# Tile 3's v moved behind the second quarter of w_in, with a planner told of later landings, in a fused local attention and squared-ReLU FFN kernel

## The chip, the cores and the metric

The kernel runs on one core of a Trainium2 chip. The metric is the device time of one execution in microseconds (us); lower is better. The core's engines run their own instruction streams and meet through semaphores: TensorE (PE in the profile; its weight loads are PEld), VectorE (DVE), ScalarE (ACT), GpSimd (POOL) and SyncE (SP). POOL, SP and ACT also issue DMA transfers, which the core's 16 DMA engines carry out.

## The reference, cut to what matters

```python
batch, n_heads, seq, head_dim = (4, 8, 768, 64)
n_global, n_local = (8, 96)
n_tokens, d_model, d_ff = (3072, 512, 2048)

scores = q @ k.T / sqrt(64)                       # per batch and head
rel = pos[:, None] - pos[None, :]
is_global = pos[None, :] < n_global
is_local = (rel >= 0) & (rel < n_local)
keep = is_global | is_local
dist = where(is_global & ~is_local, n_local, abs(rel))
scores = where(keep, scores - slope[head] * dist, -1e9)
a = softmax(scores)
x = (a @ v) as [3072 tokens, 512]                 # heads side by side
h = maximum(x @ w_in, 0)                          # w_in is 512 x 2048
out = (h * h) @ w_out                             # w_out is 2048 x 512
```

All inputs and the output are float32. The kernel works in float16 and accumulates in float32.

## The kernel before

**Tiling.** The 3072 tokens are cut into 24 tiles of 128; six tiles make one of the four sequences. A query looks at most 95 keys back and at the first 8 keys of its sequence, so a tile needs its own keys, those of the tile ahead of it (into which `fix_k` and `fix_v` copy the global keys and values) and nothing else. Attention runs tile by tile. The two layers of the FFN run on chunks, `CHUNKS = [1]*8+[2]*8`: chunks c0 to c7 are one tile each, c8 to c15 two tiles each (c9 is tiles 10 and 11).

**One tile's chain.** q and k are transposed to head-major form: in tiles 0 to 5 by TensorE (`trp`, then a copy to `qk` by `evac`), later by a DMA transpose that SP issues (L422). TensorE makes the scores `sp` (L466; 16 matmuls for the two key tiles, 8 in the first tile of a sequence), ACT takes the exponential to `ex` (L479), DVE multiplies by the mask to `ph` (L485), TensorE multiplies with v to `av` (L495), and DVE divides (`rec`, `tm`; L504 and L505). `tm` is transposed to `xt`: in tiles 0 to 5 by TensorE (`trx`, L511) and a copy, from tile 6 on by a DMA transpose on SP (L523).

**The FFN.** Layer 1 (`first`, L639) goes over 16 slices m of w_in, 128 columns each, with four matmuls per slice into `hps`; slices m0 to m3 need the first quarter of w_in, m4 to m7 the second, and so on. ACT takes the ReLU (`hr`, L647), DVE squares it (`h`, L654). Layer 2 (`second`, L660) makes `yps` in four parts, one for each quarter of w_out; DVE copies to `y`, and SP issues the store (L670).

**Loads.** All of q, k, v, w_in and w_out come by DMAs that POOL issues (L359, L395, L402), which also turn float32 to float16; only tile 0's q and k come by SP and ACT. POOL's order is the list in the last block: v of tile 0, then tiles 1 and 2, the first quarter of w_in, tile 3, the other three quarters of w_in, w_out, and the tiles from 4 on. A load waits until its buffer is free (three for q and k together, five for v).

**PSUM.** Two pools: `one`, four buffers of one bank, and `big`, two buffers of two banks. `trp`, `trx`, `av`, `yps` live in `one`; `sp` lives in `big`; `hps` lives where `home` says. A buffer is given out again in turn, when its reader has let it go.

**What sets the order.** The whole program is a list of operations with estimated durations, needs, buffers and ranks. `Plan.emit` walks through it in model time and picks for each engine the next operation whose needs are met, by rank; the pick fixes the instruction order on that engine, and on the chip each engine runs its own order, waiting at an instruction whose input is missing. `late` adds a lag to the modelled landing of POOL's loads; `SURE` and `SLACK` say how much earlier a buffer must be free, and how much later an operation may start, to be among those that are picked from; `NUDGE` shifts ranks of single stages. Where the plan foresees that TensorE idles in the first 45 us it puts in matmuls on zeros (`warm`, L269), which fill the time and compute nothing.

Of the kernel before, what the change touches and what calls it, by code (L numbers as in the profile page):

```python
# [8 lines left out]
FP32 = mybir.dt.float32  # L9
# [4 lines left out]
P = 128  # L14


class Dma:
# [34 lines left out]
class Plan:  # L52
# [115 lines left out]
                gone[key] = done  # L168

    def late(self, at):  # L170
        return 700 if at < 15500 else 1300 if at < 43000 else 0


SURE = {"PE": 0, "ACT": 60, "DVE": 60}
SLACK = {"PE": 0, "ACT": 100, "DVE": 0}


@with_exitstack
def kernel(
# [11 lines left out]
    nc = tc.nc  # L191
# [18 lines left out]
    EARLY = True  # L210


    NUDGE = {('attention', 11): -10, ('attention', 1): 10, ('attention', 13): -10, ('attention', 7): 100, ('layer 2', 1): 25, ('layer 2', 6): 100, ('attention', 8): 10, ('layer 2', 11): -100, ('attention', 3): 10, ('layer 1', 9): -100, (3.5, 1): 100, ('attention', 20): -25, (2.5, 2): 200, (2, 9): -100, ('attention', 6): 10, (4.5, 16): 25, ('layer 2', 13): -200, ('attention', 23): -200, (1.5, 4): -25, ('layer 1', 5): -10, ('layer 1', 10): -10, ('attention', 5): -200, (4, 16): -100, ('layer 2', 0): 50, ('attention', 19): -10, (2, 4): 25, ('attention', 14): 200, ('attention', 9): 50, ('layer 1', 1): 100, (2, 15): -10, (6, 11): -10, ('attention', 18): -10, ('layer 2', 15): 10, ('attention', 2): -100, ('layer 1', 0): 50, (1.5, 8): 100, (3, 3): 200, ('layer 1', 11): -50, (6, 4): 10, ('layer 1', 2): -25, ('layer 2', 8): 50, ('attention', 10): 25, (1.5, 9): 100, (4.5, 4): -10, ('layer 1', 8): 10, (4.5, 7): 100, ('layer 1', 14): 100, ('layer 1', 13): -25}

    EARLY_QK, TOUCH = ("SP","ACT"), "ACT"

    EARLY_V = None

    W_IN = 4


    ADDED = 0
# [1 line left out]
    SPLIT = {}  # L224
# [31 lines left out]
    touched = const.tile([P, NCT, 1], FP32, name="touched")  # L256
    w_out_sb = const.tile([P, NFT, d_model], FP16, name="w_out_sb")


# [14 lines left out]
    add = plan.op  # L274
# [47 lines left out]
    def constants():  # L322
        add("DVE", 120, lambda: vec.memset(blank, 0.0), rank=-999)
        add("DVE", 250, lambda: vec.tensor_scalar(
            out=ident, in0=dist[:, 0:P], scalar1=0.0, scalar2=None, op0=ALU.is_equal),
            needs=["dist"], makes=["ident"], rank=-999)
        if EARLY:
            add("DVE", 250, lambda: vec.tensor_scalar(
                out=ident32, in0=dist[:, 0:P], scalar1=0.0, scalar2=None, op0=ALU.is_equal),
                needs=["dist"], makes=["ident32"], rank=-998)  # L330
        add("DVE", 2350, fill_reach, needs=["dist"], makes=["reach"], rank=-997)
        if ADDED:
            for h in range(H):
                add("ACT", 190, lambda h=h: fill_diag(h), needs=["ident"], makes=[("diag", h)],
                    rank=-990 + h)
        for h in range(H):
            add("ACT", 420, lambda h=h: fill_mask(h), needs=["reach"], makes=[("mask", h)],
                rank=-990 + h if h < 4 else -185)


    v_bufs = [const.tile([P, H, D + 1], FP16, name=f"v{i}") for i in range(BUFS["v"])]
# [40 lines left out]
    def fetch_early_v():  # L382
        queue = {"ACT": nc.scalar, "SP": nc.sync}[EARLY_V[0]]
        add(EARLY_V[0], 450, lambda: queue.dma_start(out=early[:, 2], in_=source(0, "v")),
            makes=["ev"], rank=-998, work=920, to=210, back=1000)
        add(EARLY_V[1], 450, lambda: copy(EARLY_V[1], v_bufs[0][:, :, 0:D], early[:, 2]),
            needs=["ev", "ones"], makes=[("sv", 0)], takes=[("v", ("v", 0))], rank=-100)


    def touch_w_in():  # L390
        {"ACT": nc.scalar, "SP": nc.sync}[TOUCH].dma_start(out=touched, in_=moe_w_in[:, 0:1].rearrange("(k p) f -> p k f", p=P))

    def load_w_in(c):
        n = d_ff // W_IN
        pool_dma(745, lambda: nc.gpsimd.dma_start(  # L395
            out=w_in_sb[:, :, c * n:(c + 1) * n],
            in_=moe_w_in[:, c * n:(c + 1) * n].rearrange("(k p) f -> p k f", p=P)),
            10240 // W_IN if W_IN == 4 else 1340, makes=[("w_in", c)])

    def load_w_out(c):  # L400
        n = NFT // 4
# [127 lines left out]
    def attention(t, c, j, n, due):  # L529
# [5 lines left out]
        if t >= TURN_QK:  # L535
            add("SP", 1230, lambda: turn_by_dma(t), needs=[("sq", t), ("sk", t)],
                work=1920, to=1100, back=1000, takes=[("qk", ("qk", t))], frees=[("stage", t)], rank=due(0),
                makes=all_of("qk", t))
        else:
            for names in (("q", "k") if t == 0 else ("qk",)):  # L540
                for p in parts:
                    add("PE", 56 * len(names) * wide * (2 if t == 0 and EARLY else 1),
                        lambda names=names, p=p: turn(t, p, names),
                        needs=[("s" + x, 0, p) if t == 0 and EARLY else ("s" + x, t) for x in names]
                        + ["ident32" if t == 0 and EARLY else "ident"]
                        + ([("t", t, p, "q")] if names == "k" else []),
                        makes=[("t", t, p, names[-1])],
                        takes=[("one", ("t", t, p))] if "q" in names else [],
                        frees=[("stage", t)] if "k" in names and p == parts[-1] else [], rank=due(0))
            for p in parts:  # L550
                for x in ("qk", ) if t or not SPLIT else "qk":
                    eng = {0: 'DVE', 1: 'DVE', 2: 'DVE', 5: 'DVE', 4: 'DVE', 3: 'DVE'}.get(t, "ACT") if len(x) == 2 else SPLIT[x, parts.index(p)]
# [52 lines left out]
        for p in parts:  # L605
            tms = [("tm", t, g) for g in range(2) if len(parts) == 1 or p == parts[g]]
            takes = [("xt", ("xt", c))] if j == 0 and p[0] == 0 else []
            if t >= TURN_X:
# [4 lines left out]
            add("PE", 56 * wide, lambda p=p: to_x(t, p), needs=tms + ["ident"],  # L613
                makes=[("tx", t, p)], takes=[("one", ("tx", t, p))],
                frees=[("tm", t)] if p == parts[-1] else [], rank=due(4))
            eng = {(1, 0): 'DVE'}.get((t, parts.index(p)), "ACT")
            add(eng, 70 + (70 if eng == "DVE" else 105) * wide, lambda p=p, eng=eng: copy_x(t, c, j, p, eng),
                needs=[("tx", t, p)] + (all_of("x", t - 1) if j else [])
                + ([("x", t, parts[0])] if p != parts[0] else []),
# [4 lines left out]
        return 1 if t0 < 12 else 2  # L624

    def home(t0):
        return "one" if t0 in (0,) else "big"

    def first(c, t0, n, m):
        per = 4 // n  # L630
# [41 lines left out]
    def layer_1(c, t0, n, due):  # L672
        xs = [y for t in range(t0, t0 + n) for y in all_of("x", t)]
        per, x = 4 // n, banks(t0)
        for m in range(NFT):
            i, place = divmod(m, x * per)
            add("PE", 4 * (n * 54 + 1), lambda m=m: first(c, t0, n, m),
                needs=xs + [("w_in", m * W_IN // NFT)] + ([("l1", c, m - 1)] if m else []),
                makes=[("l1", c, m)],
                takes=([(home(t0), ("hps", c, i))] if place == 0 else [])  # L680
                + ([("h2", ("h2", c))] if m == 0 else []),
# [34 lines left out]
    with tc.manual_schedule():  # L716
# [6 lines left out]
            fetch_early()  # L723
        if EARLY_V:
            fetch_early_v()
        if TOUCH:
            add(TOUCH, 530, touch_w_in, rank=-1000, work=460, to=210, back=1000)
        for kind, n in [('v', 0), ('qkv', 1), ('qkv', 2), ('i', 0), ('qkv', 3), ('i', 1), ('i', 2), ('i', 3), ('o', 0), ('o', 1), ('o', 2), ('o', 3), ('qkv', 4), ('qkv', 5), ('qkv', 6), ('qkv', 7), ('qkv', 8), ('qkv', 9), ('qkv', 10), ('qkv', 11), ('qkv', 12), ('qkv', 13), ('qkv', 14), ('qkv', 15), ('qkv', 16), ('qkv', 17), ('qkv', 18), ('qkv', 19), ('qkv', 20), ('qkv', 21), ('qkv', 22), ('qkv', 23)]:
# [51 lines left out]
```

## Time and profile before

| | us |
|---|---|
| median of three runs | 215.76 |
| lowest and highest | 215.57, 215.81 |
| the profiled execution, by the same clock | 214.87 |
| its span, first to last instruction | 213.1 |
| TensorE busy, the `warm` matmuls among it | 205.6 |
| DVE busy | 122.1 |
| ACT busy | 102.7 |
| POOL busy | 68.1 |

The span is 1.77 us shorter than the profiled execution's own time. A row of a timeline reads: start, length, engine, source line, operation, output<-inputs, number of instructions, and in brackets the engine's idle time before and what ended it. The lengths of TensorE's rows hold the drain of the last matmul, so neighbouring rows overlap; the distance between two starts is what the first one takes. The granted clock of TensorE was 0.998 of full speed over the whole span.

### The profile page before, as it was taken

Reading aid. Unit: us, or ns where it says so; the run is one execution under the profiler, and the core shown is the slowest. Engines: PE = TensorE matmul, PEld = TensorE weight load, DVE = VectorE, ACT = ScalarE, POOL = GpSimd, SP = SyncE. Lnnn points to the kernel's source line nnn. Section 1 sums busy time; section 2 is a strip of 40 time slices with the busy share of each in tenths; the row PEclk is TensorE's granted clock in tenths of the full one; section 3 lists DMA queues with packets and bytes.
Section 4 is the critical chain, followed back from the end, with each engine's and each line's share of the span. In section 5 each row is a group of like instructions: output and inputs, shape, how many; then the busy total and the mean of one; then the engine's idle time right before and its main releaser. Section 6 shows DMA issues by size and latency. Waiting matters only on the chain.

```text
span 213.1 us, 5399 instructions
## 1 busy us (share of the span) xinstructions
PE 205.6 (96%) x2253; PEld 145.6 (68%) x2253; DVE 122.1 (57%) x296; ACT 102.7 (48%) x132; POOL 68.1 (32%) x84
## 2 busy tenths in 40 slices
PE   7869999999999999999999999999999999999994
PEld 4458986657967665875878585757676574888453
DVE  5697562774647877657566545664646674232321
ACT  4775663433764656565464635453353641345100
POOL 8975433727604544632207230451000000000000
PEclk9999999999999999999999999999999999999999
DMA  8999999999996999999939999699511222100112
GB/s 121 150 174 205 207 207 173 182 150 253 154 166 127 163 185 203 183 136 205 173 67 98 137 127 134 115 148 179 105 25 52 77 69 82 49 0 3 49 49 98
DMA packets 112232, 27.61 MB, mean 130 GB/s; under 512 B 104784, under 2 KB 109264, under 8 KB 112208
## 3 DMA queue, kind: packets, MB, share of 16 engines
q0 software_dynamic: 77024, 13.37, 87.3%
q1 hardware_dynamic: 33600, 13.64, 30.7%
q10 hardware_dynamic: 1584, 0.26, 0.7%
q8 instruction: 17, 0.28, 0.5%
q14 instruction: 7, 0.06, 0.1%
HBM read 27.27 MB, written 6.29 MB: 157 GB/s over the span
## 4 chain that ended last, share of the span: by engine, by line
PE 90%; DMA 4%; POOL 3%; DVE 1%; issue 0%
PE yps L660 40%; PE hps L639 39%; PE sp L466 5%; PE av L495 5%; DMA w_in_sb<-in_moe_w_in_dram 4%; POOL s L359 2%; POOL v L359 1%; PE trp L416 1%; PE trx L511 0%; DVE qk L429 0%; DVE tm L505 0%; PE warm L269 0%; DVE rec L504 0%; DVE y L429 0%; DVE v L442 0%
## 5 line engine op out<-in xcount | busy, mean ns | idle before, releaser
L639 PE MATMUL hps<-xt,w_in_sb 128*128 128x128 f16 (+1 forms) x1024 | 91.7, 246 | 1.0 <-DMA w_in_sb<-in_moe_w_in_dram 1.0
L660 PE MATMUL yps<-w_out_sb,h 128*128 128x512 f16 (+2 forms) x416 | 91.2, 363 | 0.0
L639 PEld LDWEIGHTS <-w_in_sb 128*128 128x128 f16 x1024 | 79.2, 98 | 12.7 <-DMA w_in_sb<-in_moe_w_in_dram 1.2
L647 ACT ACTIVATE hr<-hps 128x512 f16<-128x512 f32 (+1 forms) x72 | 52.7, 739 | 68.5 <-PE hps L639 64.9
L660 PEld LDWEIGHTS <-h 128*128 128x128 f16 x416 | 37.0, 98 | 34.8 <-DVE h L654 0.4
L654 DVE TENSOR_TENSOR h<-hr 128x512 f16<-128x512 f16 (+1 forms) x72 | 36.7, 511 | 38.8 <-ACT hr L647 38.6
L479 ACT ACTIVATE ex<-sp 128x1024 f16<-128x1024 f32 (+1 forms) x45 | 42.9, 1002 | 20.0 <-PE sp L466 19.9
L359 POOL DMA_DIRECT2D v<-in_v_dram x24 | 21.5, 896 | 64.1 <-issue 19.7
L485 DVE TENSOR_TENSOR ph<-ex,mask 128x1024 f16<-128x1024 f16 (+1 forms) x45 | 30.0, 676 | 14.1 <-ACT ex L479 13.9
L429 DVE COPY y<-yps 128x512 f32<-128x512 f32 (+2 forms) x26 | 16.9, 648 | 20.0 <-PE yps L660 19.7
L359 POOL DMA_DIRECT2D s<-in_q_dram x23 | 20.5, 891 | 7.9 <-PE hps L639 2.4
L359 POOL DMA_DIRECT2D s<-in_k_dram x23 | 20.7, 898 | 4.6 <-DMA w_out_sb<-in_moe_w_out_dram 2.9
L505 DVE TENSOR_TENSOR tm<-av,rec 128x256 f16<-128x256 f32 x48 | 20.4, 424 | 1.7
L495 PE MATMUL av<-v,ph 128*128 128x65 f16 x352 | 15.0, 193 | 1.0 <-DVE ph L485 1.0
L466 PEld LDWEIGHTS <-qk 64*128 64x128 f16 x352 | 9.9, 94 | 8.7 <-issue 5.9
L495 PEld LDWEIGHTS <-ph 128*128 128x128 f16 x352 | 13.6, 97 | 3.1 <-DVE ph L485 1.4
L466 PE MATMUL sp<-qk 64*128 64x128 f16 x352 | 14.2, 218 | 0.5 <-DVE qk L429 0.2
L504 DVE RECIPROCAL rec<-av 128x4 f32<-128x4 f32 x48 | 8.5, 176 | 9.3 <-PE av L495 9.2
L269 PE MATMUL warm<-blank 128*128 128x256 f16 x37 | 7.7, 317 | 1.2 <-DVE v L345 1.2
L439 DVE COPY qk<-qk 128x128 f16<-128x128 f16 x16 | 4.8, 302 | 1.2 <-PE sp L466 0.6
L427 ACT COPY xt<-trx 128x512 f16<-128x512 f16 (+1 forms) x6 | 3.1, 515 | 4.9 <-PE trx L511 4.9
L269 PEld LDWEIGHTS <-blank 128*128 128x128 f16 x37 | 3.8, 113 | 2.1 <-DVE v L345 1.2
(32 smaller groups left out, 38.1 us busy)
## 6 DMA issues: line engine op xcount, KB each, us to landing
out_dram<-y SPq DMA_DIRECT2D x23, 256.0 KB, 3.4
v<-in_v_dram POOLq DMA_DIRECT2D x24, 128.0 KB, 5.0
s<-in_q_dram POOLq DMA_DIRECT2D x23, 128.0 KB, 5.3
s<-in_k_dram POOLq DMA_DIRECT2D x23, 128.0 KB, 5.9
w_in_sb<-in_moe_w_in_dram POOLq DMA_DIRECT2D x4, 512.0 KB, 10.1
w_out_sb<-in_moe_w_out_dram POOLq DMA_DIRECT2D x4, 512.0 KB, 15.9
qk<-s SPq DMA_TRANSPOSE x18, 6.0
xt<-tm SPq DMA_TRANSPOSE x18, 4.6
```

The lines of the kernel that those rows point to most:

```text
L269: nc.tensor.matmul(to[:, 0:2 * P], lhsT=blank[:, 0:P], rhs=blank[:, 0:2 * P], start=True, stop=True)
L359: nc.gpsimd.dma_start(out=dst, in_=source(t, name))
L429: vec.tensor_copy(out=out, in_=src)
L466: nc.tensor.matmul(live["sp", t, before, part][:, e, a, :], lhsT=live["qk", t - before][rows, 1, a, :], rhs=live["qk", t][rows, 0, a, :], ...
L479: nc.scalar.activation(out=some(live["ph" if t < ADDED else "ex", t, before], part), in_=some(live["sp", t, before, part], part), func=AF. ...
L485: vec.tensor_tensor(out=some(live["ph", t, before], part), in0=some(live["ex", t, before], part), in1=some(mask[:, kind], part), op=ALU.mult)
L495: nc.tensor.matmul(av[:, i, :], lhsT=live["ph", t, before][:, h % 2, h // 2, :], rhs=v_bufs[(t - before) % len(v_bufs)][:, h, :], start=be ...
L505: vec.tensor_tensor(out=live["tm", t][:, 4 * g:4 * g + 4, :], in0=av[:, :, 0:D], in1=rec[:, :, None].to_broadcast([P, 4, D]), op=ALU.mult)
L639: nc.tensor.matmul(live["hps", c, i][:, w, o * n * P:(o + 1) * n * P], lhsT=w_in_sb[:, kk, m * P:(m + 1) * P], rhs=live["xt", c][:, kk, 0: ...
L647: nc.scalar.activation(out=hr[:, 0:x, 0:w], in_=live["hps", c, i][:, 0:x, 0:w], func=AF.Relu)
L654: vec.tensor_tensor(out=to, in0=hr, in1=hr, op=ALU.mult)
L660: nc.tensor.matmul(live["y", c, j, cols][:, 0:cols[1] - cols[0]], lhsT=live["h2", c][:, m, j * P:(j + 1) * P], rhs=w_out_sb[:, m, cols[0]: ...
```

## The change

Tile 3's loads are cut in two: its q and k stay ahead of the second quarter of w_in, its v goes behind it. `late` tells the planner of lags of 0.7 us to 11.5 us and of 1.6 us to 43 us (before: 0.7 to 15.5 us, 1.3 to 43 us). `home` puts the layer 1 outputs of tile 1 into single banks as well as those of tile 0. `SURE` and `SLACK`, the ranks in `NUDGE` and the offset of the attention's ranks get other numbers. All eight masks are filled ahead of the first exponential; single copies change their engine (tile 0's first half and tiles 2 and 5 of `xt` to DVE, tile 1's to ACT; tile 4's `qk` to ACT). The rest of the diff writes `W_IN` and the early touch of w_in in a more general form with the same transfers.

```diff
     def late(self, at):
-        return 700 if at < 15500 else 1300 if at < 43000 else 0
+        return 700 if at < 11500 else 1600 if at < 43000 else 0
...
-SURE = {"PE": 0, "ACT": 60, "DVE": 60}
-SLACK = {"PE": 0, "ACT": 100, "DVE": 0}
+SURE = {"PE": 0, "ACT": 0, "DVE": 0}
+SLACK = {"PE": 0, "ACT": 60, "DVE": 60}
...
-    NUDGE = {('attention', 11): -10, ('attention', 1): 10, ...
+    NUDGE = {('attention', 7): 100, ('layer 2', 1): -200, ...
...
-                rank=-990 + h if h < 4 else -185)
+                rank=-990 + h)
...
     def load_w_in(c):
-        n = d_ff // W_IN
+        at = slice(sum(W_IN[:c]) * P, sum(W_IN[:c + 1]) * P)
         pool_dma(745, lambda: nc.gpsimd.dma_start(
-            out=w_in_sb[:, :, c * n:(c + 1) * n],
-            in_=moe_w_in[:, c * n:(c + 1) * n].rearrange("(k p) f -> p k f", p=P)),
-            10240 // W_IN if W_IN == 4 else 1340, makes=[("w_in", c)])
+            out=w_in_sb[:, :, at], in_=moe_w_in[:, at].rearrange("(k p) f -> p k f", p=P)),
+            200 + 590 * W_IN[c], makes=[("w_in", c)])
...
-                    eng = {0: 'DVE', 1: 'DVE', 2: 'DVE', 5: 'DVE', 4: 'DVE', 3: 'DVE'}.get(t, "ACT") ...
+                    eng = {0: 'DVE', 1: 'DVE', 2: 'DVE', 5: 'DVE', 6: 'DVE', 3: 'DVE'}.get(t, "ACT") ...
...
-            eng = {(1, 0): 'DVE'}.get((t, parts.index(p)), "ACT")
+            eng = {(0, 0): 'DVE', (2, 0): 'DVE', (5, 0): 'DVE'}.get((t, parts.index(p)), "ACT")
...
     def home(t0):
-        return "one" if t0 in (0,) else "big"
+        return "one" if t0 in (0,1) else "big"
...
-        for kind, n in [('v', 0), ('qkv', 1), ('qkv', 2), ('i', 0), ('qkv', 3), ('i', 1), ('i', 2), ('i', 3), ...
+        for kind, n in [('v', 0), ('qkv', 1), ('qkv', 2), ('i', 0), ('qk', 3), ('i', 1), ('v', 3), ('i', 2), ('i', 3), ...
...
-                          100 * (t0 - n + j) + 6 * st - 100
+                          100 * (t0 - n + j) + 6 * st - 80
```

What it moves is seen in the instruction orders. First POOL, from the first quarter of w_in on; `v_114` before and `v_113` after are the buffer of tile 3's v. Before:

```order
L395 DMA w_in_sb<-in_moe_w_in_dram 128x4x512
L359 DMA s<-in_q_dram 128x8x64
L359 DMA s<-in_k_dram 128x8x64
L359 DMA v_114<-in_v_dram 128x8x64
L395 DMA w_in_sb<-in_moe_w_in_dram 128x4x512 x3
L402 DMA w_out_sb<-in_moe_w_out_dram 128x4x512 x4
```

Now:

```order
L401 DMA w_in_sb<-in_moe_w_in_dram 128x4x512
L359 DMA s<-in_q_dram 128x8x64
L359 DMA s<-in_k_dram 128x8x64
L401 DMA w_in_sb<-in_moe_w_in_dram 128x4x512
L359 DMA v_113<-in_v_dram 128x8x64
L401 DMA w_in_sb<-in_moe_w_in_dram 128x4x512 x2
L407 DMA w_out_sb<-in_moe_w_out_dram 128x4x512 x4
```

One quarter of w_in has changed places with tile 3's v; the other loads stand where they stood.

Second TensorE, from the first layer 1 matmul to the first one that needs the second quarter of w_in; of each group the first matmul is shown. `xt_243` before and `xt_287` after belong to tile 0, `xt_406` and `xt_379` to tile 1. Before, the last row is where slice m4 of c0 begins:

```order
L639 MATMUL hps_357<-xt_243,w_in_sb_108 128x128
...
L511 MATMUL trx_383<-ident_100,tm_350 128x128
...
L269 MATMUL warm_393<-blank_106 128x256
...
L416 MATMUL trp_396<-ident_100,s_228 128x128
...
L495 MATMUL av_408<-v2_113,ph_381 128x65
...
L639 MATMUL hps_432<-xt_406,w_in_sb_108 128x128
...
L269 MATMUL warm_459<-blank_106 128x256
...
L511 MATMUL trx_462<-ident_100,tm_427 128x128
...
L466 MATMUL sp_472<-qk_457 128x128
...
L269 MATMUL warm_493<-blank_106 128x256
...
L639 MATMUL hps_495<-xt_243,w_in_sb_108 128x128
```

Now, where `hps_483` is slice m4 of c0:

```order
L516 MATMUL trx_365<-ident_100,tm_350 128x128
...
L644 MATMUL hps_373<-xt_287,w_in_sb_108 128x128
...
L644 MATMUL hps_396<-xt_379,w_in_sb_108 128x128
...
L500 MATMUL av_408<-v2_112,ph_370 128x65
...
L421 MATMUL trp_427<-ident_100,s_221 128x128
...
L471 MATMUL sp_456<-qk_449 128x128
...
L516 MATMUL trx_476<-ident_100,tm_437 128x128
...
L644 MATMUL hps_483<-xt_287,w_in_sb_108 128x128
...
L644 MATMUL hps_507<-xt_379,w_in_sb_108 128x128
```

The transposes of tile 1's `tm` have moved ahead of layer 1, the four `warm` groups between the two quarters are gone, and the rest between the two quarters (32 layer 1 matmuls of tiles 0 and 1, 16 `av` and 4 `trx` of tile 2, 8 `trp` and 16 `sp` of tile 3) is the same in another order (between the `trp` and the `sp` stand the last two slices of `hps_396`).

Third SP, where the `xt` of chunk c9 (tiles 10 and 11) is transposed; `xt_1750` before and `xt_1752` after are c9's, the second row of each is tile 11's. Before:

```order
L523 DMA_TRANSPOSE xt_1750<-tm_1717 128x4x128
L422 DMA_TRANSPOSE qk_1778<-s_1638 128x8x128
L670 DMA out_0_dram<-y_1797 128x512
L422 DMA_TRANSPOSE qk_1870<-s_1756 128x8x128
L523 DMA_TRANSPOSE xt_1750<-tm_1815 128x4x128
L523 DMA_TRANSPOSE xt_1932<-tm_1890 128x4x128
```

Now:

```order
L528 DMA_TRANSPOSE xt_1752<-tm_1720 128x4x128
L427 DMA_TRANSPOSE qk_1765<-s_1652 128x8x128
L675 DMA out_0_dram<-y_1773 128x512
L528 DMA_TRANSPOSE xt_1752<-tm_1851 128x4x128
L427 DMA_TRANSPOSE qk_1896<-s_1763 128x8x128
L528 DMA_TRANSPOSE xt_1978<-tm_1963 128x4x128
```

Tile 11's `xt` no longer stands behind the transpose of tile 15's q and k.

More of the change, by code (lines that the diff above doesn't have):

```diff
@@ L210 @@
     EARLY = True
-    NUDGE = {('attention', 11): -10, ('attention', 1): 10, ('attention', 13): -10, ('attention', 7): 100, ('layer 2', 1): 25, ('layer 2', 6): 100, ('attention', 8): 10, ('layer 2', 11): -100, ('attention', 3): 10, ('layer 1', 9): -100, (3.5, 1): 100, ('attention', 20): -25, (2.5, 2): 200, (2, 9): -100, ('attention', 6): 10, (4.5, 16): 25, ('layer 2', 13): -200, ('attention', 23): -200, (1.5, 4): -25, ('layer 1', 5): -10, ('layer 1', 10): -10, ('attention', 5): -200, (4, 16): -100, ('layer 2', 0): 50, ('attention', 19): -10, (2, 4): 25, ('attention', 14): 200, ('attention', 9): 50, ('layer 1', 1): 100, (2, 15): -10, (6, 11): -10, ('attention', 18): -10, ('layer 2', 15): 10, ('attention', 2): -100, ('layer 1', 0): 50, (1.5, 8): 100, (3, 3): 200, ('layer 1', 11): -50, (6, 4): 10, ('layer 1', 2): -25, ('layer 2', 8): 50, ('attention', 10): 25, (1.5, 9): 100, (4.5, 4): -10, ('layer 1', 8): 10, (4.5, 7): 100, ('layer 1', 14): 100, ('layer 1', 13): -25}
-    EARLY_QK, TOUCH = ("SP","ACT"), "ACT"
+    NUDGE = {('attention', 7): 100, ('layer 2', 1): -200, ('attention', 8): -25, ('layer 2', 11): 100, ('attention', 3): -50, ('layer 1', 9): 50, (2.5, 2): 200, (2, 9): -100, (4.5, 16): 25, ('layer 2', 13): -200, (1.5, 4): -25, ('layer 1', 5): 100, ('layer 1', 10): 100, ('attention', 5): -200, (4, 16): -100, ('layer 2', 0): 50, ('attention', 19): -10, (2, 4): 25, ('attention', 14): 50, ('attention', 9): 50, ('layer 1', 1): 10, (2, 15): -10, (6, 11): -10, ('attention', 18): -10, ('layer 1', 0): -100, (1.5, 8): 100, (3, 3): 200, ('layer 1', 11): -50, (6, 4): -100, ('layer 2', 8): 100, ('attention', 10): 25, (1.5, 9): 100, (4.5, 4): -10, (4.5, 7): 100, ('layer 1', 13): 25, (2.5, 4): 200, (0.5, 12): -10, ('attention', 4): 10, ('layer 2', 10): 100, (2.5, 14): -100, ('attention', 12): 50, (4.5, 5): -200, (0.5, 4): -10, (6, 10): 50, ('layer 1', 2): 50, (1.5, 6): 10, (3, 23): 50, (1.5, 1): -100, (6, 8): 100, ('layer 1', 4): 50, ('layer 1', 6): 50, ('layer 2', 5): -50, (3.5, 6): -200, ('attention', 21): 50, (3.5, 14): 100, ('attention', 2): 50, (2.5, 12): -50, ('attention', 6): 50, (3.5, 4): 10, ('layer 1', 12): -25, (3, 11): 50, (0, 20): 25, ('attention', 11): 25, (3.5, 9): 200, ('layer 1', 3): 10, ('layer 1', 14): 50}
+    EARLY_QK = ("SP","ACT")
+    TOUCH = (("ACT", ()),)
     EARLY_V = None
-    W_IN = 4
+    W_IN = (4,) * 4
     ADDED = 0
@@ L255 @@
     w_in_sb = const.tile([P, NCT, d_ff], FP16, name="w_in_sb")
-    touched = const.tile([P, NCT, 1], FP32, name="touched")
     w_out_sb = const.tile([P, NFT, d_model], FP16, name="w_out_sb")
@@ L386, in fetch_early_v, with touch_w_in @@
         add(EARLY_V[1], 450, lambda: copy(EARLY_V[1], v_bufs[0][:, :, 0:D], early[:, 2]),
-            needs=["ev", "ones"], makes=[("sv", 0)], takes=[("v", ("v", 0))], rank=-100)
-    def touch_w_in():
-        {"ACT": nc.scalar, "SP": nc.sync}[TOUCH].dma_start(out=touched, in_=moe_w_in[:, 0:1].rearrange("(k p) f -> p k f", p=P))
+            needs=["ev", "ones"], makes=[("sv", 0)], takes=[("v", ("v", 0))], rank=200)
+    def touch_w_in(queue, behind):
+        to = const.tile([P, NCT, 1], FP32, name="touched")
+        if behind:
+            add("DVE", 60, lambda: vec.memset(to, 0.0), needs=behind, makes=["touch"], rank=-1000)
+        add(queue, 530, lambda: {"ACT": nc.scalar, "SP": nc.sync}[queue].dma_start(
+            out=to, in_=moe_w_in[:, 0:1].rearrange("(k p) f -> p k f", p=P)),
+            needs=["touch"] if behind else [], rank=-1000, work=460, to=210, back=1000)
     def load_w_in(c):
-        n = d_ff // W_IN
+        at = slice(sum(W_IN[:c]) * P, sum(W_IN[:c + 1]) * P)
         pool_dma(745, lambda: nc.gpsimd.dma_start(
-            out=w_in_sb[:, :, c * n:(c + 1) * n],
-            in_=moe_w_in[:, c * n:(c + 1) * n].rearrange("(k p) f -> p k f", p=P)),
-            10240 // W_IN if W_IN == 4 else 1340, makes=[("w_in", c)])
+            out=w_in_sb[:, :, at], in_=moe_w_in[:, at].rearrange("(k p) f -> p k f", p=P)),
+            200 + 590 * W_IN[c], makes=[("w_in", c)])
     def load_w_out(c):
@@ L551, in attention @@
                 for x in ("qk", ) if t or not SPLIT else "qk":
-                    eng = {0: 'DVE', 1: 'DVE', 2: 'DVE', 5: 'DVE', 4: 'DVE', 3: 'DVE'}.get(t, "ACT") if len(x) == 2 else SPLIT[x, parts.index(p)]
+                    eng = {0: 'DVE', 1: 'DVE', 2: 'DVE', 5: 'DVE', 6: 'DVE', 3: 'DVE'}.get(t, "ACT") if len(x) == 2 else SPLIT[x, parts.index(p)]
                     add(eng, (600 if t else 615) * wide // (4 if t else 2) if eng == "DVE"
@@ L677, in layer_1 @@
             add("PE", 4 * (n * 54 + 1), lambda m=m: first(c, t0, n, m),
-                needs=xs + [("w_in", m * W_IN // NFT)] + ([("l1", c, m - 1)] if m else []),
+                needs=xs + [("w_in", [c for c, n in enumerate(W_IN) for _ in range(n)][m])] + ([("l1", c, m - 1)] if m else []),
                 makes=[("l1", c, m)],
@@ L725 @@
             fetch_early_v()
-        if TOUCH:
-            add(TOUCH, 530, touch_w_in, rank=-1000, work=460, to=210, back=1000)
-        for kind, n in [('v', 0), ('qkv', 1), ('qkv', 2), ('i', 0), ('qkv', 3), ('i', 1), ('i', 2), ('i', 3), ('o', 0), ('o', 1), ('o', 2), ('o', 3), ('qkv', 4), ('qkv', 5), ('qkv', 6), ('qkv', 7), ('qkv', 8), ('qkv', 9), ('qkv', 10), ('qkv', 11), ('qkv', 12), ('qkv', 13), ('qkv', 14), ('qkv', 15), ('qkv', 16), ('qkv', 17), ('qkv', 18), ('qkv', 19), ('qkv', 20), ('qkv', 21), ('qkv', 22), ('qkv', 23)]:
+        for queue, behind in TOUCH:
+            touch_w_in(queue, behind)
+        for kind, n in [('v', 0), ('qkv', 1), ('qkv', 2), ('i', 0), ('qk', 3), ('i', 1), ('v', 3), ('i', 2), ('i', 3), ('o', 0), ('o', 1), ('o', 2), ('o', 3), ('qkv', 4), ('qkv', 5), ('qkv', 6), ('qkv', 7), ('qkv', 8), ('qkv', 9), ('qkv', 10), ('qkv', 11), ('qkv', 12), ('qkv', 13), ('qkv', 14), ('qkv', 15), ('qkv', 16), ('qkv', 17), ('qkv', 18), ('qkv', 19), ('qkv', 20), ('qkv', 21), ('qkv', 22), ('qkv', 23)]:
             if kind in "io":
```

## The prediction

> **What bounds the kernel now.** I read the page first: the busy times, and who holds the chain that ended last.
>
> ```profile
> PE 205.6 (96%) x2253; PEld 145.6 (68%) x2253; DVE 122.1 (57%) x296; ACT 102.7 (48%) x132; POOL 68.1 (32%) x84
> PE 90%; DMA 4%; POOL 3%; DVE 1%; issue 0%
> ```
>
> TensorE holds the chain for 90%. What is not TensorE lies at the start: the chain of waits goes by POOL's issues to the landing of w_in's first quarter, and behind it the chain is TensorE alone until the last outputs. So a gain must come from the first 20 us, and a loss can come from any place where the new order makes TensorE wait. The timeline of TensorE from the first layer 1 matmul on:
>
> ```profile
> 15.28 1.07 PE L639 MATMUL hps<-xt,w_in_sb 128*128 128x128 f16 x16 [1.03 <-DMA w_in_sb<-in_moe_w_in_dram]
> 16.18 0.39 PE L511 MATMUL trx<-ident,tm 128*128 128x128 f16 x4
> 16.40 0.38 PE L269 MATMUL warm<-blank 128*128 128x256 f16 x2
> 16.62 0.72 PE L416 MATMUL trp<-ident,s 128*128 128x128 f16 x8
> 17.18 0.65 PE L495 MATMUL av<-v,ph 128*128 128x65 f16 x16
> 17.66 1.06 PE L639 MATMUL hps<-xt,w_in_sb 128*128 128x128 f16 x16
> 18.56 0.38 PE L269 MATMUL warm<-blank 128*128 128x256 f16 x2
> 18.77 0.57 PE L511 MATMUL trx<-ident,tm 128*128 128x128 f16 x4
> 19.18 0.27 PE L269 MATMUL warm<-blank 128*128 128x256 f16 x1
> 19.66 0.62 PE L466 MATMUL sp<-qk 64*128 64x128 f16 x16 [0.20 <-DVE qk L429]
> 20.21 0.28 PE L269 MATMUL warm<-blank 128*128 128x256 f16 x1
> 20.36 7.32 PE L639 MATMUL hps<-xt,w_in_sb 128*128 128x128 f16 x128
> 27.52 0.65 PE L495 MATMUL av<-v,ph 128*128 128x65 f16 x16
> ```
>
> From start to start: 16 narrow `hps` take 0.90 us, 128 take 7.16 (0.056 each), 16 `av` 0.48, 4 `trx` 0.22, 16 `sp` 0.55. From 20.36 TensorE is full; before it `warm` and idle time lie between the groups. The 20.36 is set by a DMA, as the landings of the loads show; each pair of rows is one load, its issue and its time to landing:
>
> ```profile
> L359 POOL DMA_DIRECT2D s<-in_k_dram x1: 947/947/947, 9.3 to 9.3; - x1
> DMA to landing us min/median/max: 7.6/7.6/7.6
> ...
> L359 POOL DMA_DIRECT2D v<-in_v_dram x1: 956/956/956, 10.2 to 10.2; - x1
> DMA to landing us min/median/max: 7.7/7.7/7.7
> ...
> L395 POOL DMA_DIRECT2D w_in_sb<-in_moe_w_in_dram x1: 842/842/842, 11.1 to 11.1; - x1
> DMA to landing us min/median/max: 9.3/9.3/9.3
> ...
> L402 POOL DMA_DIRECT2D w_out_sb<-in_moe_w_out_dram x1: 742/742/742, 17.2 to 17.2; - x1
> DMA to landing us min/median/max: 18.6/18.6/18.6
> ```
>
> Tile 3's k lands at 16.9, its v at 17.9, the second quarter of w_in at 20.4 (TensorE's start at 20.36 cuts the rounding), w_out's last quarter at 35.8. POOL issued the first three within 1.8 us of each other and 7.6 to 9.3 us ahead: they land in the order of issue, one behind another, and the queue is what is full. In it v takes 17.9 - 16.9 = 1.0 and a quarter of w_in 2.5.
>
> **The change part by part.**
>
> *The swapped loads.* The second quarter now follows k: 16.9 + 2.5 = 19.4, so it lands 0.96 earlier (20.36 against 19.40). v lands behind it at 20.36, 2.46 later than before. All later loads stand behind the same bytes and keep their times. POOL's own work is the same; both issues are far ahead of the landing.
>
> *Who waits for v.* Its first `av` stands in the new order behind 60 narrow `hps` after the second quarter's first: 19.40 + 60 x 0.056 = 22.75, 2.4 after v's landing. The lateness is covered by this layer 1 work. Without that cover it would cost up to those 2.4.
>
> *Is TensorE ready at 19.40?* Between the two quarters stand, besides the removed `warm`, the same groups as before but for `trx` of tile 1, now ahead of the first quarter. From 15.28: 16 `hps` 0.90, 8 `hps` 0.45, `av` 0.48, `trp` at most 0.56, 8 `hps` 0.45: 18.12 at the latest (the `av` start at 16.63, 0.55 earlier than before). Then `sp` and `trx` need DVE, whose rows for this tile were:
>
> ```profile
> 17.62 0.18 DVE L504 RECIPROCAL rec<-av 128x4 f32<-128x4 f32 x1 [0.19 <-PE av L495]
> 17.84 0.42 DVE L505 TENSOR_TENSOR tm<-av,rec 128x256 f16<-128x256 f32 x1
> 18.18 0.27 DVE L442 COPY v<-v 32x520 f16<-32x520 f16 x1
> 18.38 0.16 DVE L504 RECIPROCAL rec<-av 128x4 f32<-128x4 f32 x1
> 18.58 0.42 DVE L505 TENSOR_TENSOR tm<-av,rec 128x256 f16<-128x256 f32 x1
> 18.92 0.68 DVE L429 COPY qk<-trp 128x1024 f16<-128x1024 f16 x1
> ```
>
> `rec` began 0.44 after `av`, and all six took 1.98. Now `qk` comes third and the v copy last. `av` at 16.63 gives `rec` 17.07 and `tm` to 17.65; the `trp` are through at about 17.75, so `qk` runs to 18.45, `sp` 18.5 to 19.05, and the second `tm` is done at 19.0: `trx` 19.05 to 19.27, 0.1 ahead of the landing. At worst `sp` waits for all of DVE's steps but the v copy (16.63 + 2.48 - 0.20 = 18.9) and `trx` ends at 19.7: 0.3 of the gain gone. If DVE is quicker nothing more is won, since the landing holds. I take the landing, 0.96.
>
> *What follows.* The order goes through all of w_in earlier, so I count up to w_out's last quarter: 188 narrow `hps` (10.5), 16 `av` in two groups (0.52), 4 `trx` (0.22) and 24 `yps` (24 x 0.216 = 5.19; 8 of them take 1.73 in the chain below) end at 19.40 + 16.4 = 35.8, just when it lands. No quarter comes after its use, but a start much before 19.4 would be worth nothing. Between 0 and 0.1 lost; I take 0.
>
> *Single banks for tile 1, other ranks and engines.* The counts of matmuls are equal but for three fewer `warm`. The only shape that differs from then on: two more tiles have their 16 `av` as 8 and 8. The chain of waits in order of time prices it, and the pieces of a rival:
>
> ```profile
> 74.79 0.48 PE av L495 x16
> ...
> 84.49 0.33 PE sp L466 x8
> ...
> 86.28 3.93 PE hps L639 x36
> 90.21 0.26 PE av L495 x8
> ...
> 102.23 6.99 PE hps L639 x64
> ...
> 120.96 1.83 PE yps L660 x8
> ...
> 129.38 1.73 PE yps L660 x8
> ```
>
> 2 x (2 x 0.26 - 0.48) = 0.08 lost. The two more masks ahead of the first exponential and tile 0's other order fall before 15.28, where TensorE idled 1.03 us. The rest is the order of ACT and DVE (48% and 57% busy): free while no buffer comes late, from nothing up to the rival below.
>
> *Sum.* -0.96 + 0.08 = -0.88 on the profiled execution's 214.87 (span 213.1 and 1.77 around it): 213.99. That execution is 0.89 under the median of the runs; on the median 215.76 the same difference gives **214.9**.
>
> **The rivals.**
>
> *A new wait at chunk c9 (slower).* In the new order c9's first matmul comes soon after tile 11's last `av`: 24 wide `hps` (24 x 3.93/36 = 2.62), 8 `sp` 0.33, 8 `yps` 1.83, 16 `sp` 0.55, 8 `av` 0.26 with about 0.1 behind the `sp`, 8 `yps` 1.73: 7.4 us. Before it was 15.9 (tile 11's `av` ended at 86.28, c9 began at 102.23). In them DVE must divide and SP's transpose must land:
>
> ```profile
> 76.76 1.19 SPq L523 DMA_TRANSPOSE xt<-tm  x1
> ...
> 91.51 3.58 SPq L523 DMA_TRANSPOSE xt<-tm  x2
> ...
> DMA to landing us min/median/max: 5.1/5.1/5.1
> ...
> DMA to landing us min/median/max: 2.4/4.6/8.3
> ```
>
> Tile 9's `xt` was issued at 76.76, 1.5 after its `av` ended (75.27), and took 5.1 (the first landing row; the second is that of all 18). That leaves 5.9 for the landing. For: in this very stage the slowest took 8.3, which would stop TensorE for 2.4: 217.3. Against: that one was issued at 91.51, behind tile 15's transpose, which it now precedes; tile 9's 5.1 and the median 4.6 fit. It makes the kernel slower than the bound once the landing takes over 5.9 + 0.88 + 0.43 = 7.2. The Trainium skill has a rule for it (DMA: Bandwidth & Descriptors, Queues, rings and completion order): each DMA engine takes a packet from one queue, then from the next that has work. By it SP's transpose shares the engines with the loads that POOL issues when tile 11's v goes free, and every load in flight stretches it. The trace agrees as far as it goes, with 2.4 to 8.3 for transposes of one size. With the rule the time lies anywhere from 214.9 to 217.3, without it at the forecast.
>
> *TensorE or DVE is not ready.* If the 0.3 of DVE's bound comes, and tile 1's `trx`, now ahead of layer 1, still has to run when the first quarter has landed (0.22, its row at 16.18), the gain shrinks to 0.36: 215.4.
>
> *The change doesn't do what it says.* If order in POOL's queue didn't set the landing, the quarter would still come at 20.36, and only the 0.08 would stay: 215.84. Against it: three landings in the order of issue, spaced by their size.
>
> **How the numbers follow.** Forecast 0.60, with its own range 214.5 to 215.2 (a little more or less queue time, 0.1 at each landing); c9 0.21, between 214.9 and 217.3 by the landing; not ready 0.11; no shift 0.08. The 80% range takes in the forecast, the two small rivals and the lower half of c9's: 214.4 to 216.3. A difference of 0.2% (0.43 us) is about what a measurement of this kernel tells from none. Faster: 0.60, 0.05 of "not ready", 0.04 of c9, 0.69. Within: 0.06, 0.06 of "no shift" and 0.04 of c9, 0.16. Slower: 0.13 of c9 and 0.02 of "no shift", 0.15.
>
> **What would show it.** The second quarter of w_in lands at 19.3 to 19.5 and tile 3's v at 20.3 to 20.5; TensorE's idle before slice m4 of c0 is set by that landing, not by DVE; no `warm` after 15.3; tile 3's `av` wait for no DMA; every later chunk but c9 starts some 0.9 earlier for the same work done. If c9's first matmul waits for `xt`, the rival holds. If some other wait of TensorE over 0.2 us appears after 20 us, the reading that the new order is free was wrong.

## The result, and the profile after

| | before | after |
|---|---|---|
| median of 22 runs each, us | 215.71 | 214.25 |
| lowest and highest | 214.55, 217.06 | 213.30, 216.96 |
| the profiled execution | 214.87 | 214.21 |
| its span | 213.1 | 212.4 |

The ratio after to before is 0.9936, with an interval of 0.9917 to 0.9956: the kernel became faster, by 1.46 us between the medians. (The ratios, and the medians and ranges of the experiments below, leave out executions over 1.5% above the fastest of their kernel; the table has one such, 216.96.) The two profiled executions lie only 0.66 apart; where the rest is will need more traces than these two.

The profile page of the changed kernel, its busy line and the shares of the chain that ended last:

```profile
PE 205.4 (97%) x2250; PEld 145.9 (69%) x2250; DVE 121.5 (57%) x297; ACT 102.7 (48%) x131; POOL 68.2 (32%) x84
PE 81%; DMA 9%; issue 3%; DVE 3%; POOL 1%; SPq 1%; ACT 0%; POOLq 0%
```

TensorE is as busy as before, yet its share of the chain has fallen from 90% to 81%: the chain now leaves TensorE somewhere behind the start. The start first, in the timeline of TensorE:

```profile
15.04 1.51 PE L644 MATMUL hps<-xt,w_in_sb 128*128 128x128 f16 x24
16.39 0.65 PE L500 MATMUL av<-v,ph 128*128 128x65 f16 x16
16.87 0.61 PE L421 MATMUL trp<-ident,s 128*128 128x128 f16 x8
17.32 0.61 PE L644 MATMUL hps<-xt,w_in_sb 128*128 128x128 f16 x8
18.40 0.62 PE L471 MATMUL sp<-qk 64*128 64x128 f16 x16 [0.47 <-DVE qk L434]
18.95 0.40 PE L516 MATMUL trx<-ident,tm 128*128 128x128 f16 x4
19.30 3.52 PE L644 MATMUL hps<-xt,w_in_sb 128*128 128x128 f16 x60
22.66 0.32 PE L500 MATMUL av<-v,ph 128*128 128x65 f16 x5
```

Slice m4 of c0 begins at 19.30 where it began at 20.36: 1.06 earlier. The two loads that changed places, each with its issue and its time to landing; first the second quarter of w_in, then tile 3's v:

```profile
L401 POOL DMA_DIRECT2D w_in_sb<-in_moe_w_in_dram x1: 828/828/828, 10.2 to 10.2; - x1
DMA to landing us min/median/max: 9.0/9.0/9.0
...
L359 POOL DMA_DIRECT2D v<-in_v_dram x1: 968/968/968, 11.0 to 11.0; - x1
DMA to landing us min/median/max: 9.3/9.3/9.3
```

The quarter lands at 19.25 by the trace's finer clock and v at 20.23, 2.4 ahead of its first use at 22.66. Then the place where the chain leaves TensorE, in the chain of waits (start, length, what held it):

```profile
120.73 0.87 POOL v L359
121.61 0.34 POOL s L359
121.95 0.52 issue
122.46 7.92 DMA s<-in_k_dram
...
130.52 1.23 SPq L427
...
131.84 7.15 DMA xt<-tm
138.99 0.14 issue
139.13 0.92 PE hps L644 x7
```

At 139.13 the first layer 1 matmul of chunk c12 waits for the `xt` of tile 17. On TensorE itself:

```profile
138.26 0.42 PE L500 MATMUL av<-v,ph 128*128 128x65 f16 x8
139.13 1.14 PE L644 MATMUL hps<-xt,w_in_sb 128*128 128x256 f16 x9 [0.44 <-DMA xt<-tm]
```

Eight `av` take 0.26 from start to start, so the matmul could have begun at 138.52; it lost 0.61. This `xt` was issued on SP behind the transpose of tile 21's q and k, and that one stood there until tile 21's k had landed at 130.38. In the kernel before, tile 17's `xt` (the last row) stands behind the same transpose (the first row), but comes due 3.9 us later:

```profile
132.88 1.23 SPq L422 DMA_TRANSPOSE qk<-s  x1
134.25 0.49 SPq L670 DMA_DIRECT2D out_dram<-y  x1
136.74 1.19 SPq L523 DMA_TRANSPOSE xt<-tm  x1
```

It landed at 141.93, 1.05 before c12 began at 142.98. In the new order tile 17's `av` begins 6.4 us earlier (128.65 for 135.08), but tile 21's k lands only 2.4 earlier (130.38 for 132.74), so the two transposes now meet on SP.

So 1.06 was won at the start and 0.61 given back at 139 us; smaller gaps that the old order has and the new one lacks make another 0.2, and the spans differ by 0.7.

### The profile page after: what moved, and what is told of

Read it like the earlier page. It is cut to its first block, busy times and chain, and to the rows that moved or that the text cites. A ratio compares the mean times of both kernels' runs of the same rounds, so it can differ in the third digit from the quotient of the medians.

```text
span 212.4 us, 5388 instructions
## 1 busy us (share of the span) xinstructions
PE 205.4 (97%) x2250; PEld 145.9 (69%) x2250; DVE 121.5 (57%) x297; ACT 102.7 (48%) x131; POOL 68.2 (32%) x84
## 4 chain that ended last, share of the span: by engine, by line
PE 81%; DMA 9%; issue 3%; DVE 3%; POOL 1%; SPq 1%; ACT 0%; POOLq 0%
PE yps L665 36%; PE hps L644 34%; DMA s<-in_k_dram 6%; PE sp L471 5%; PE av L500 4%; DMA xt<-tm 3%; DVE qk L434 1%; POOL v L359 1%; PE trp L421 1%; PE trx L516 1%; DVE tm L510 1%; SPq L427 1%; POOL s L359 1%; DVE ph L490 0%; ACT hr L652 0%
## 5 line engine op out<-in xcount | busy, mean ns | idle before, releaser
L644 PE MATMUL hps<-xt,w_in_sb 128*128 128x128 f16 (+1 forms) x1024 | 92.7, 246 | 0.4 <-DMA xt<-tm 0.4
L269 PE MATMUL warm<-blank 128*128 128x256 f16 x34 | 7.0, 333 | 1.2 <-DVE v L345 1.2
L447 DVE COPY v<-v 32x520 f16<-32x520 f16 x16 | 4.4, 274 | 0.0
L444 DVE COPY qk<-qk 128x128 f16<-128x128 f16 x16 | 3.9, 246 | 0.7 <-PE sp L471 0.3
```

Source lines behind the costliest of these rows:

```text
L269: nc.tensor.matmul(to[:, 0:2 * P], lhsT=blank[:, 0:P], rhs=blank[:, 0:2 * P], start=True, stop=True)
L644: nc.tensor.matmul(live["hps", c, i][:, w, o * n * P:(o + 1) * n * P], lhsT=w_in_sb[:, kk, m * P:(m + 1) * P], rhs=live["xt", c][:, kk, 0: ...
```

## The experiments

Three theories stood. A: the earlier landing of the second quarter is the gain. B: the kernel before loses time in most executions at a place that its first trace does not show, and the new order has removed that place. C: the changed kernel gives part of its gain back at c12. Each kernel had 12 runs, but for the two with tile 17's `xt` first, which had 6. Kernels on one chip share the runs of the kernel before: the first four had 34 of them (median 215.43), the next four 29 (215.5), the last three 23 (215.71).

### The swap alone, forwards and backwards

Four kernels: the two as they are, and each with only the two loads exchanged, every engine's order otherwise its own.

```diff
+        one, other = (next(i for i, op in enumerate(plan.ops) if m in op[4])
+                      for m in (("w_in", 1), ("sv", 3)))
+        for i, fn in ((one, plan.ops[other][2]), (other, plan.ops[one][2])):
+            plan.ops[i] = plan.ops[i][:2] + (fn,) + plan.ops[i][3:]
```

The kernel before, unchanged:

> The kernel before, once more. Theory A (the swap of the loads explains the gain; the rest of the 1.46 us is scatter of single executions): its ratio to the kernel before is 1.000, and a second trace again shows TensorE full from the second quarter of w_in on, span 213 to 214. Theory B (most executions of the kernel before also wait later on, in places that the first traced execution was spared): a trace with a span of about 214 has at least one wait of TensorE of over 0.3 us after 20.4 us, at a transpose or a load that lands late.

Measured: 215.1 (214.48 to 217.15), ratio 0.9987 [0.9954, 1.002].

The changed kernel with v ahead of the quarter again:

> The changed kernel with all its engines' orders, but tile 3's v and the second quarter of w_in put back in the order of before. Theory A: slice m4 of chunk c0 begins at 20.2 to 20.4 in place of 19.3, and the time rises by 1.0 us, to about 215.2. Theory B: the same 1.0 us is lost at that place, and 0.4 to 0.5 us of gain on the kernel before stays, since it comes from the order later on. If the new orders alone were the gain, the time would stay near 214.3.

Measured: 214.59 (213.99 to 216.11), ratio 0.9956 [0.9928, 0.9984].

The kernel before with v behind the quarter:

> The kernel before with its engines' orders, and tile 3's v behind the second quarter of w_in. Theory A and B: the quarter lands near 19.3, but TensorE's own order reaches slice m4 only at 20.3 (warm matmuls and a wait for DVE lie ahead), so 0.0 to 0.15 us is won and the time is 215.6. A rival, that the swap alone makes the gain: 0.9 us or more is won.

Measured: 215.3 (214.66 to 216.52), ratio 0.9995 [0.9965, 1.0026].

The changed kernel, unchanged:

> The changed kernel once more. Both theories: 214.25, ratio 0.993 to 0.994, with the second quarter of w_in at 19.2 to 19.4. Theory B: a second trace may show the wait of chunk c12 for tile 17's transpose (0.4 us in the first) in another size, 0 to 1.5 us.

Measured: 214.12 (213.21 to 215.2), ratio 0.9919 [0.989, 0.9949].

Slice m4 in the second of these (the changed kernel, v ahead), in TensorE's timeline, with the group ahead of it:

```profile
19.52 0.40 PE L516 MATMUL trx<-ident,tm 128*128 128x128 f16 x4
20.69 0.40 PE L644 MATMUL hps<-xt,w_in_sb 128*128 128x128 f16 x4 [0.77 <-DMA w_in_sb<-in_moe_w_in_dram]
```

TensorE is through at 19.7 and waits for the landing at 20.64: with v ahead it is the load that holds, as theory A says. The third (the kernel before, v behind):

```profile
19.01 0.27 PE L269 MATMUL warm<-blank 128*128 128x256 f16 x1
19.49 0.62 PE L466 MATMUL sp<-qk 64*128 64x128 f16 x16 [0.20 <-DVE qk L429]
20.04 0.28 PE L269 MATMUL warm<-blank 128*128 128x256 f16 x1
20.16 0.94 PE L639 MATMUL hps<-xt,w_in_sb 128*128 128x128 f16 x14
```

Here the quarter had landed at 19.73, and TensorE came to it only at 20.16, behind `sp`, which waits for DVE's `qk`, and a `warm`. So the old order can hardly use an earlier landing, and the swap alone is worth nothing that these runs can tell: 215.3 beside 215.1 and 215.43. The traces of the old order with v ahead say the same: the quarter landed between 19.60 and 20.31, and in three of the five TensorE reached m4 only 0.26 to 0.39 behind the landing; in the other two it waited for the landing 0.03 and 0.23. In the changed kernel the swap is worth 0.47 (214.59 less 214.12), half of what theory A forecasts. The landing alone is not the gain: 0.84 (215.43 less 214.59) remains with v back in its old place, where theory B forecast 0.4 to 0.5.

### Where the kernel before loses time

The trace of the unchanged kernel in this first group shows, in TensorE's timeline, a wait that the trace the prediction was read from does not have; it is the first layer 1 matmul of chunk c6:

```profile
60.12 1.90 PE L660 MATMUL yps<-w_out_sb,h 128*128 128x512 f16 x8
62.47 0.90 PE L639 MATMUL hps<-xt,w_in_sb 128*128 128x128 f16 x13 [0.45 <-DMA xt<-tm]
```

Eight `yps` take 1.74, so 0.61 is lost to tile 6's `xt`, issued at 55.32 and landed at 62.42. In the first trace the same transpose was issued at 55.72 and took 5.83, where the order leaves it 6.53: c6 began at 62.25 without a wait. The changed kernel has 16 layer 1 matmuls of c5 ahead of c6's first, and in its first trace 7.5 us (55.50 to 63.02). The edit moves the first 16 layer 1 matmuls of c6 behind four more `yps` of tile 4 (0.86 us) in the kernel before, and changes no other order:

```diff
+        def hold(early, late):
+            held = []
+            for i, op in enumerate(plan.ops):
+                if any(m in op[4] for m in early):
+                    fn = lambda fn=op[2]: held.append(fn)
+                elif late in op[4]:
+                    fn = lambda fn=op[2]: [f() for f in (fn, *held)]
+                else:
+                    continue
+                plan.ops[i] = op[:2] + (fn,) + op[3:]
+        hold([("l1", 6, m) for m in range(4)], ("l2", 4, 0, (0, d_model), 3))
```

> The kernel before, with the first four slices of chunk c6 (16 matmuls) moved behind the four layer 2 matmuls that follow them, so that tile 6's xt has 0.86 us more to land. Theory B (most executions of the kernel before wait there, 0.6 us in its second trace): 0.3 to 0.6 us won, about 215.1 where the kernel before has 215.5. Theory A (no such wait in most executions): 0.0, within 0.2 us of the kernel before.

Measured: 215.0 (214.78 to 215.57), ratio 0.9991 [0.997, 1.0012]. Beside it once more the unchanged kernel:

> The kernel before, for a third trace. Theory B: again at least one wait of TensorE of 0.3 us or more after 20.4 us at c6's xt or at a quarter of w_in. Theory A: none, as in the first trace, and a time that follows the landing of the second quarter alone.

Measured: 216.08 (214.78 to 216.93), ratio 1.0022 [0.9997, 1.0048]. Its trace has the wait again, more than twice as long:

```profile
60.36 1.90 PE L660 MATMUL yps<-w_out_sb,h 128*128 128x512 f16 x8
63.40 1.07 PE L639 MATMUL hps<-xt,w_in_sb 128*128 128x128 f16 x16 [1.14 <-DMA xt<-tm]
```

The transpose (issued at 55.57) took 7.8 here, and 1.30 is lost. In the edited kernel:

```profile
60.15 2.76 PE L660 MATMUL yps<-w_out_sb,h 128*128 128x512 f16 x12
62.75 1.06 PE L639 MATMUL hps<-xt,w_in_sb 128*128 128x128 f16 x16
```

No wait, though its `xt` landed at 62.34, 0.45 later than the old place (60.15 + 1.74) would have needed it. The same edit on another chip:

> The kernel before with c6's first four slices 0.86 us later, again. Theory B: its runs are 214.8 to 215.6 as in the first sample, without the kernel before's runs of 216 to 218, a median 0.4 to 0.6 us below it. Theory A: the same spread as the kernel before.

Measured: 215.24 (214.74 to 216.05), ratio 0.9982 [0.9958, 1.0005]. Both medians lie about 0.5 under that of the kernel before on their chip (215.0 to 215.5, 215.24 to 215.71; but the unchanged kernel's other sample on the first of these chips, 216.08, lies 0.58 above its 215.5), and the long runs are gone (highest 215.57 and 216.05, where the kernel before reached 217.18 and 217.17). Six traces of this order agree in size: the transpose took 5.4 to 7.8, and what it took above 6.5 is 0.43 on the mean. But both ratios' intervals take in 1. The edit also has a small cost of its own: in both its traces the 16 `av` near 68 us take 0.71 from start to start (67.90 to 68.61 in the first), where the kernel before takes 0.48. That the wait exists and that the edit removes it is shown; that it is worth some 0.4 to 0.5 is likely, not settled. One trace shows how narrow the new order's room is: in the changed kernel with v ahead the transpose took 7.5, and landed at 64.42 where c6 was due at 64.41.

### Where the changed kernel gives time back

In the changed kernel, tile 17's `xt` is put ahead of the transpose of tile 21's q and k on SP, with `hold` as above, and nothing else:

```diff
+        hold(all_of("qk", 21), all_of("x", 17)[0])
```

> The changed kernel, with tile 17's xt transposed on SP ahead of tile 21's q and k. Theory C (the changed kernel gives part of the swap's 0.96 us back at chunk c12, whose xt stands behind a transpose that waits for tile 21's k): the wait of 0.4 to 0.6 us at c12 is gone, xt lands near 137, time 213.6 to 213.8. Rival: xt is late for the traffic, not for its place; the wait stays and so does 214.2.

Measured: 213.55 (213.17 to 213.79), ratio 0.9919 [0.9893, 0.9946]. SP's timeline:

```profile
130.51 1.19 SPq L528 DMA_TRANSPOSE xt<-tm  x1
131.87 1.25 SPq L427 DMA_TRANSPOSE qk<-s  x1
```

TensorE's at c12:

```profile
138.47 0.42 PE L500 MATMUL av<-v,ph 128*128 128x65 f16 x8
138.72 1.25 PE L644 MATMUL hps<-xt,w_in_sb 128*128 128x256 f16 x10
```

The `xt` went out 1.33 earlier, landed at 135.54, and the wait is gone. What is moved behind it costs nothing: TensorE does not wait for tile 21's `qk`. The same with the two loads exchanged as well, so that v is ahead:

> The same as the run before, with tile 3's v and the second quarter of w_in in the order of before. Theory C: with the wait at c12 gone the swap is worth its whole 0.9 to 1.0 us, so this is 0.9 to 1.0 us slower than the run with v behind, about 214.6. If the swap is worth only the 0.47 us that the first pair showed, the difference stays 0.5.

Measured: 214.55 (213.92 to 215.62), ratio 0.9953 [0.9924, 0.9983]. Slice m4 began at 20.33 there and at 18.98 in the one before. With c12 out of the way the swap is worth 1.0 (214.55 less 213.55), close to the 0.96 that the queue gives. The traces of the group above show why it may have been worth only 0.47 there: the changed kernel waited 0.40 at c12, and the one with v ahead did not, since its `xt` landed at 138.97 and TensorE came late enough not to wait for it. The medians alone, of 6 to 12 runs that scatter by up to 2 us, would not tell 0.47 from 1.0.

The changed kernel a third time and the one with `xt` first once more, on the third chip:

> The changed kernel beside the next two on one chip. Theory C: a median of 214.1 to 214.3 with a wait of 0.3 to 0.7 us at chunk c12 for xt in the trace.

Measured: 214.27 (213.18 to 215.25), ratio 0.9932 [0.9906, 0.9957].

> The changed kernel with tile 17's xt ahead of tile 21's transpose on SP, again. Theory C: 0.4 to 0.6 us faster than the changed kernel on the same chip, 213.5 to 213.8, with no wait at c12. If its first median was luck of that chip, it equals the changed kernel.

Measured: 213.84 (213.19 to 214.03), ratio 0.9904 [0.9878, 0.9929]. The difference is 0.43 on this chip, after 0.57 between two chips (214.12 on the first, 213.55 on the second). The ratios to the kernel before do not settle its size: 0.9919 for both on the first two chips, and 0.9932 and 0.9904 with overlapping intervals on the third. But none of the twelve runs with `xt` first is over 214.03, where 25 of the 44 of the changed kernel are. The mechanism of theory C is shown: all three traces of the changed kernel have the wait, 0.61, 0.40 and 0.36 (the second has `av` at 138.17 and c12 at 138.83, the third 139.58 and 140.19), and neither trace of it with `xt` first has it. This version beats the kernel before (0.9919 and 0.9904 with the intervals given), and by its medians the changed kernel too.

### What adds up and what stays open

Three traces of each kernel give a sum to hold against the forecast. The kernel before began m4 at 20.36, 19.65 and 20.03, the changed one at 19.30, 18.94 and 19.65: 0.72 earlier on the mean. c6 cost the first 0, 0.61 and 1.30 (mean 0.64), c12 the second 0.45. Waits for the fourth quarter of w_in, which comes late in some executions, took 0.25 of the one and 0.40 of the other. Smaller gaps in the old order that the new one lacks make 0.12. Together -0.72 - 0.64 + 0.45 + 0.15 - 0.12 = -0.88; the mean spans differ by 0.89 (213.56 and 212.67). So these six traces are explained. The medians of many runs differ by 1.46, 1.31 and 1.44 where both ran; three traces of each, whose spans scatter over 1.2 and 1.4, can't tell where the remaining 0.4 to 0.6 lies. The pair with neither the swap nor these two waits differs by 0.45: 214.55 (new order, v ahead, `xt` first) against 215.0 (old order, c6 later) on the same chip. About half of that can be the second one's own cost at 68 us; a place for the rest is not shown. That stays open. The new order can be late elsewhere, too: with `xt` first, one trace has `sp` waiting 0.46 for a `qk` transpose at 50.95.

## Why the prediction was right and where it failed

Forecast was a difference of -0.88 and a median of 214.9, in a range from 214.4; the median is 214.25, and lies under the range. The direction and the main mechanism held, the size did not.

*The swapped loads.* Right in the first trace: 19.25 for 19.40, and 20.23 for v's 20.36, the later loads 0.2 to 0.4 earlier. In time, with c12 out of the way, it is 1.0 for 0.96. The 20.36 that it starts from is one trace's, and even there TensorE waited for the landing only some 0.03: its last `warm` began at 20.21, and the third trace of the kernel before, where the landing is early, has 0.12 from this `warm` to m4 (19.91 to 20.03). Over the five traces of each order with its own sequence of loads, m4 began at 20.08 and 19.30 on the mean, 0.78 apart. The three landings also are not "spaced by their size": v has a quarter of the bytes (128 KB to 512 KB) and took 1.0 of the quarter's 2.5.

*Who waits for v.* Right: the first `av` of tile 3 at 22.66 waits for nothing.

*Is TensorE ready at 19.40?* Right: `av` at 16.39, `sp` at 18.40 (forecast 18.5), `trx` at 18.95, and the landing sets the start, by 0.1. The third experiment adds what the prediction saw only as a list of groups: this readiness is the new order's doing. Without it the swap is worth nothing that these runs can tell.

*What follows.* Right for the bytes: no wait for w_in or w_out in this trace. In two other executions the fourth quarter of w_in came late by 0.25 and 0.95.

*Single banks.* The +0.08 does not show in the sum: from m4 to the last matmul the new order takes 189.18 in two of the three traces that have no wait there (189.24 in the third), and 189.40 in the first trace of the kernel before. Other small gaps of the old order went at the same time, so whether the 0.08 is in it stays open.

*"Free while no buffer comes late, from nothing up to the rival below".* This failed, though not where the rival put it. A buffer does come late, but in c12, not in c9. At c9 tile 11's `xt` was behind no transpose that waited for a load, issued at 90.02 and landed at 94.97, 1.3 before c9 began at 96.27; it took 5.0 of the 6.25 that were left (the rival said 5.9):

```profile
L528 SPq DMA_TRANSPOSE xt<-tm x1: 1754/1754/1754, 90.0 to 90.0; - x1
...
DMA to landing us min/median/max: 5.0/5.0/5.0
```

The prediction's own test ("some other wait of TensorE over 0.2 us after 20 us") catches it. The mechanism of the rival, a transpose that is late on SP, was the right kind; I looked at one chunk of the ten whose `xt` SP transposes and not at the others. SP's order alone would not have shown it, since tile 17's `xt` stands behind the transpose of tile 21 in both kernels; what moved is when each comes due, `av` of tile 17 by 6.4 us and tile 21's k by 2.4. It cost 0.36 to 0.61 in three traces.

*"On the median 215.76 the same difference gives 214.9".* This is the step that put the number outside. It takes the profiled execution, 0.89 under the median, for a usual one and lets all that the others lose stand in the new order too. The traced execution was one in which tile 6's transpose came in time. Two more traces lost 0.61 and 1.30 at c6, the new order has 7.5 us for that transpose in place of 6.5 and loses next to nothing: a gain of some 0.4 that no row of the trace could show as a loss, but that its margin could, 5.8 taken of 6.5. The two misses have opposite signs and nearly cancel, so it is luck that the six traces again add up to the forecast 0.88; the part of the median's 1.46 that neither explains is the one left open above.

*No shift; TensorE or DVE not ready.* Neither happened.

## What to carry to other kernels

An execution that lies under the median by more than the effect you forecast is a lucky one: list the transfers whose spare time is below their own scatter, and price what the change does to each of them, even where the trace shows no wait. A load that is moved forward pays only if the engine behind it is ready that early, so look at the swap and the order as one. When a planner writes a new order, go through every in-order issue queue for an issue that now comes due while the one ahead of it still waits for a late input; their order need not have changed, and here it had not. One such place gave back about half of what the earlier load was worth, and with the two issues exchanged the wait was gone.

## What the runs showed of the hardware

The same load, issued at the same time, does not land at the same time. The first quarter of w_in, in the kernel after and in the kernel before a second time:

```profile
L401 POOL DMA_DIRECT2D w_in_sb<-in_moe_w_in_dram x1: 804/804/804, 7.7 to 7.7; - x1
DMA to landing us min/median/max: 7.3/7.3/7.3
```

```profile
L395 POOL DMA_DIRECT2D w_in_sb<-in_moe_w_in_dram x1: 809/809/809, 7.7 to 7.7; - x1
DMA to landing us min/median/max: 6.1/6.1/6.1
```

Over 13 traces it landed between 13.81 and 15.56. All seven of the new order have it at 14.52 or later, five of the six of the old order at 14.36 or earlier; no run here shows why. The step from the third to the fourth quarter, 2.5 to 2.6 us in seven of the traces, was 2.3 to 3.2 in five and 3.7 in one, which cost TensorE 0.95.

Of the two transposes that meet on SP at 130.5 us, the second takes longer, whichever it is: `xt` behind `qk` took 7.1 and `qk` 5.0 (issued 130.52, landed 135.55); in the other order `xt` took 5.0 and `qk` 6.4 (131.87 to 138.27). In all seven traces of the new order the second took longer, by 0.8 to 2.4 us. This agrees with the Trainium skill (DMA: Bandwidth & Descriptors, Two DMAs through the same engine are not ordered), by which the descriptors of one queue start in order. How much longer the same transpose takes as the second, 1.4 us for `qk` and 2.1 us for `xt` here, stands in the runs alone.
